# A first state in one transfer, low halves of w_out on GpSimd, and a new opening order in an attention-and-FFN kernel

## The chip, the cores and the metric

The kernel runs on one core of one Trainium2 chip. The metric is the device time of one execution in microseconds. A core has a tensor engine (TensorE, PE in the profile; PEld is its weight load), a vector engine (VectorE, DVE), a scalar engine (ScalarE, ACT), a Pool engine (GpSimd, POOL), and a queue that issues transfers (SyncE, SP). Each engine works off its own list in order and waits on semaphores for the others.

## What is computed

```python
def _attn_ref(x, state):  # (8, 8, 512, 64), (8, 8, 32, 64)
    scores = scale * np.matmul(x, state.transpose(0, 1, 3, 2))
    ...
    xread = np.matmul(a, state)
    scores2 = scale * np.matmul(state, x.transpose(0, 1, 3, 2))
    ...
    sread = np.matmul(a2, x)
    return np.concatenate([xread, sread], axis=2).astype(np.float32)

def _moe_ref(x, w_in, w_out):  # (4352, 512), (512, 2048), (2048, 512)
    h = x @ w_in
    relu6 = np.clip(h + 3.0, 0.0, 6.0)
    g = h * relu6 / 6.0
    return (g @ w_out).astype(np.float32)
```

Left out are the two softmaxes: that of `scores` over the 32 states of a head, that of `scores2` over its 512 tokens. The heads of the attention's result are laid side by side, so that 8 x 544 rows of 512 go through the feed-forward part. The two weights arrive as 64-bit floats, and the kernel turns their digits into 32-bit floats itself.

## The kernel before

**Stages.** For each of eight batches the kernel computes softmax weights of tokens over states, and a product w' of the state with `w_in` (function `wprime`, line 512 makes its matmuls), so that `a @ state @ w_in` becomes `a @ w'`. A step n of the main loop takes 128 of the 2048 hidden columns: `first(n)` multiplies w' with the weights into a PSUM bank `ps_h`, ScalarE (line 1027) and VectorE (line 1029) form g, and `second(n)`, two steps later, multiplies g with 128 rows of `w_out` into four accumulators `acc0` to `acc3`. Most products are made of three 32-bit products of high and low halves (line 967); `split` (lines 306 and 307) makes the halves: ScalarE rounds to the high half, VectorE subtracts. The very first step takes 32-bit operands as they are (`PLAIN = 1`): line 997 in `first`, line 1046 in `second`. A ninth pass over the state's own rows ends the kernel.

**Weights.** `weight()` loads a tile of 64-bit numbers (line 373) and decodes it: ScalarE casts the upper digits (`upper`, line 382), VectorE joins the lower ones (`join`, line 387). For `w_out`, ScalarE then rounds the high half (line 414) and VectorE subtracts for the low half (line 416). This happens once, mostly during the first batch.

**The opening, batch 0.** `load_x` issues x in four quarters of two heads (line 481), and behind the first `load_state` issues the state in two transfers of 32 KB, one for each of two groups of heads, in runs of 256 bytes (line 438). `take_in` turns the state on TensorE (line 593), copies it to `stT` on ScalarE (line 599), and spreads it over the zeroed `apart` in four VectorE copies (line 606); it turns each quarter of x (line 621, eight halves of 128 columns into one bank) and ScalarE copies it out (line 625). `tokens_by_rows` makes for each quarter q the scores (line 688), VectorE the maximum (699) and the difference (707), ScalarE the exponential (710), VectorE the sum (713). After each second quarter VectorE takes the reciprocal (718) and scales the pair (720). When all is scaled, TensorE turns the weights back in two groups of four (729), one copied out by ScalarE (731) and one by VectorE (732), and line 997 can begin.

**What sets the order.** Every piece of work is put into a `Plan` with its engine (T TensorE, V VectorE, S ScalarE, Q transfers), an assumed duration, a rank, what it reads and writes, and the buffers it holds. `order()` lays them out against assumed clocks; the first several hundred follow the list `OPENING`, by numbers in the order of `plan.add`. A transfer is assumed to land at `channel + 1.6`, where the channel starts 1.3 after the issue and moves 330 KB a microsecond. `issue()` emits the work in that order, and fills assumed gaps of TensorE before the first product with idle matmuls of a constant (line 1267), one for each 0.22 us until `WARM`, and one for each 0.13 after it; before `WARM` TensorE's work is assumed to take twice as long. In the list before, SP issues x quarter 0, the state, x quarter 1, a `w_out` tile, x quarters 3 and 2, then three transfers of `w_in` (two of one tile, one of two) and two of `w_out`.

Of the kernel before, what the change touches and what calls it, by code (L numbers as in the profile page):

```python
# [35 lines left out]
PLAIN = 1  # L36

# [31 lines left out]
class Plan:  # L69
# [5 lines left out]
    AFTER = {"T": 0.25, "V": 0.12, "S": 0.12, "Q": 0.0}  # L75
    WARM = 4.5
# [26 lines left out]
    def order(self):  # L103
# [13 lines left out]
        open_ops = {e: set() for e in "TVSQ"}  # L117
# [3 lines left out]
        clock = dict.fromkeys("TVSQ", 0.0)  # L121
# [4 lines left out]
        while len(row) < n_ops:  # L126
# [65 lines left out]
    def issue(self, tc, idle, until):  # L192

        with tc.manual_schedule(
            engines={ENGINE.PE, ENGINE.DVE, ENGINE.Activation, ENGINE.SP}
        ):
# [12 lines left out]
def tile_state_attention_then_hardswish_ffn(  # L209
# [8 lines left out]
    nc = tc.nc  # L218
# [35 lines left out]
    make_identity(nc, ident)  # L254
    three = cpool.tile([P, 1], F32, name="three")
# [32 lines left out]
    def S_(cost, rank, do, reads=(), writes=(), after=()):  # L288
        return plan.add("S", cost, rank, do, reads, writes, after)

# [48 lines left out]
    def weight(kind, k, n, place, rank, load_rank):  # L339
# [68 lines left out]
        def halves(rank):  # L408

            gone = [  # L410
                m for slot, users in plan.users.items() for m in users
                if slot[1] != "home" and slot[0] in (at_home["hi"][0][0], at_home["lo"][0][0])
            ]
            S_((0.6, 1.05)[n - 1], rank, lambda: nc.scalar.copy(w_out_of("hi", k, n), low()),
               lo_keys, at_home["hi"], gone)
            V(wide, rank, lambda: nc.vector.tensor_tensor(
                w_out_of("lo", k, n), low(),
                w_out_of("hi", k, n).bitcast(F32),
                op=ALU.subtract), [*lo_keys, *at_home["hi"]], at_home["lo"])
# [10 lines left out]
    first_exps = []  # L430

    def load_state(b, rank, after=()):
        key = ("st_raw", b)

        def load():
            raw = get(key, lambda: att.tile([P, NG, D], F32, name="st_raw", bufs=1))
            for u in range(NG):
                nc.sync.dma_start(raw[:, u, :], st_v[b, :, :, u, :])  # L438
# [149 lines left out]
    def take_in(b, rank, after=(), banks=None):  # L588
# [3 lines left out]
        if b < TURNED:  # L592
            T(0.12, rank[0], lambda: nc.tensor.transpose(
                bank(st)[:, :P], made["st_raw", b].rearrange("p u d -> p (u d)"), ident),
                [("st_raw", b)], [st], after)

        def put_state():
            stT = get(("stT", b), lambda: att.tile([P, P], F32, name="stT"))
            nc.scalar.copy(stT, bank(st)[:, :P])
        if b < TURNED:  # L600
            S_(0.22, RANKS["apart"] if b == 0 else URGENT, put_state, [st], [("stT", b)])
        for u in range(NG) if b < TURNED else ():
            for i in range(2):
                def put(u=u, i=i):
                    src = bank(st)[u * D : (u + 1) * D, :P].rearrange("p (q n) -> p q n", n=NS)
                    nc.vector.tensor_copy(apart[i * D : (i + 1) * D, :, u, i], src)
                V(0.22, RANKS["apart"] if b == 0 else URGENT, put, [st], [("apart", b, u, i)])
# [19 lines left out]
    def apart_parts(b):  # L627
        return [("apart", b, u, i) for u in range(NG) for i in range(2)]
# [39 lines left out]
    def tokens_by_rows(after, banks):  # L668
# [11 lines left out]
        for q in range(NQ):  # L680
# [20 lines left out]
            if q in ():  # L701
# [13 lines left out]
            if q % 2 == 0:  # L715
# [4 lines left out]
            V(0.62, r[4], lambda pair=pair, total=total: nc.vector.tensor_tensor(  # L720
                a_by_rows().rearrange("p (a q n) -> p a q n", q=NQ, n=NS)[:, :, pair], whole[:, :, pair, :NS],
                total(pair).unsqueeze(3).to_broadcast([P, A, NG, NS]), op=ALU.mult),
                [sum_key, (*bt_key, q - 1), part_key], [("w_in2", "a", "rows", q)])
        for g in range(NG):
            back = (banks[g], ("B", 0, g))

            def turn(back=back, g=g):
                for j in range(J):
                    nc.tensor.transpose(bank(back)[:, place(j)], a_by_rows()[:, place(j * NG + g)], ident)  # L729
            T(0.47, RANKS["turn0"][0], turn, [("w_in2", "a", "rows", q) for q in (1, 3)], [back], after)  # L730
            copy = (lambda g=g, back=back: nc.scalar.copy(a_first(g), bank(back)),
                    lambda g=g, back=back: nc.vector.tensor_copy(a_first(g), bank(back)))[g]
            (S_, V)[g](0.6, RANKS["turn0"][1 + g], copy, [back], [("w_in2", "a", g)])
# [7 lines left out]
    def halves_of_first(rank):  # L741
        for g in range(NG):
            split(rank, lambda g=g: made["aT", 0]["hi"]()[:, g], lambda g=g: made["aT", 0]["lo"]()[:, g],
                  lambda g=g: a_first(g), [("w_in2", "a", g)],
# [98 lines left out]
    def place(k):  # L843
        return slice(k * P, (k + 1) * P)
# [56 lines left out]
    def put(c, ps, cols):  # L901
# [3 lines left out]
            [n for k, n in scores_at.items() if k in (0, ("L", 0))])  # L905
# [66 lines left out]
    def first(n):  # L972
        b, i, _, _ = steps[n]
        ps = ("ps_h", n)
        if b < B:
# [8 lines left out]
            if plain(b, i):  # L984
                by_group = {g: [("w_in2", "a", g), (*PLAIN_WP, f0, g)] for g in wide}
# [312 lines left out]
```

## Time and profile before

| | |
|---|---|
| median of 3 runs | 647.14 us (646.94 to 649.2) |
| span of the profiled execution | 648.4 us |
| PE busy | 640.2 us, 99% |
| DVE busy | 393.1 us, 61% |
| ACT busy | 292.3 us, 45% |
| POOL busy | 1.3 us, 8 instructions |
| mean granted TensorE clock | 0.993 |

The profile is of one execution, whose span, 648.4 us, is its own time. Its times count from the start of the span. Busy times of TensorE are modelled ends of pipelined matmuls, so a busy TensorE may still be slow. The granted clock is a share of full speed. In a row of instructions, `xb<-in_x_dram` is written tile from read tile; a bracket or the last column tells how long the engine stood idle and what ended that. In a row of transfers the last number is the time from issue to landing.

### The profile page before, as it was taken

The numbers are of one execution on the slowest core, as the hardware profiler recorded it, in microseconds if no ns is written. First come the engines' busy times: TensorE is split into PE (matmuls) and PEld (weight loads), VectorE is DVE, ScalarE is ACT, GpSimd is POOL, SyncE is SP. The second block draws the span as 40 slices with busy tenths as digits, with TensorE's granted clock in tenths as the row PEclk, the third lists the DMA queues.
The fourth block names the chain that finished last, engine by engine and source line by source line (L and its number), as shares of the span: only waits on it lengthen the run. The fifth ranks groups of instructions, "written<-read, shape, count | busy, mean of one in ns | idle before, by whom it ended". The sixth has DMA issues, their size and how long they took to land.

```text
span 648.4 us, 9867 instructions
## 1 busy us (share of the span) xinstructions
PE 640.2 (99%) x3924; PEld 502.9 (78%) x3924; DVE 393.1 (61%) x678; ACT 292.3 (45%) x509; POOL 1.3 (0%) x8
## 2 busy tenths in 40 slices
PE   8999999999999999999999999999999999999997
PEld 7577778777878777787778787787778787888996
DVE  4989995387586356834595366834694444443552
ACT  3998664335344344534344344433353343433442
POOL 0000000000000000000000000000000000000000
PEclk7999999999999999999999999999999999999999
DMA  8789302644531405041231405050232001000101
GB/s 283 264 266 257 123 2 42 110 114 73 115 66 19 79 1 135 2 73 25 70 66 28 70 2 135 7 83 9 76 57 32 1 21 46 0 1 1 65 1 33
DMA packets 135270, 46.25 MB, mean 71 GB/s; under 512 B 123576, under 2 KB 129208, under 8 KB 135096
## 3 DMA queue, kind: packets, MB, share of 16 engines
q1 hardware_dynamic: 135224, 45.62, 29.1%
q8 instruction: 31, 0.51, 0.3%
q14 instruction: 15, 0.12, 0.1%
HBM read 33.02 MB, written 8.91 MB: 65 GB/s over the span
## 4 chain that ended last, share of the span: by engine, by line
PE 97%; DMA 1%; DVE 1%; SPq 0%; issue 0%; ACT 0%
PE acc L967 58%; PE ps_h L967 30%; PE ps_s L512 4%; PE ps_h L512 2%; PE ps_h L924 1%; DMA xb<-in_x_dram 1%; PE acc L1046 1%; PE ps_s L688 1%; PE acc L621 0%; PE ps_h L997 0%; SPq L438 0%; PE acc L688 0%; DVE w_in L720 0%; PE acc L729 0%; PE ps_s L924 0%; PE acc L512 0%
## 5 line engine op out<-in xcount | busy, mean ns | idle before, releaser
L967 PE MATMUL acc<-w_out_hi,g_hi 128*128 128x512 f32 x540 | 213.3, 395 | 0.0
L967 PE MATMUL acc<-w_out_lo,g_hi 128*128 128x512 f32 x540 | 210.5, 390 | 0.0
L967 PE MATMUL acc<-w_out_hi,g_lo 128*128 128x512 f32 x540 | 210.2, 389 | 0.0
L1027 ACT ACTIVATE g<-ps_h,three 128x512 f32<-128x512 f32 (+1 forms) x144 | 95.5, 665 | 225.7 <-PE ps_h L967 221.5
L1029 DVE SCALAR_TENSOR_TENSOR g<-g,ps_h 128x512 f32<-128x512 f32 (+1 forms) x144 | 94.5, 657 | 150.1 <-ACT g L1027 149.2
L967 PEld LDWEIGHTS acc<-w_out_hi,g_hi 128*128 128x128 f32 x540 | 101.4, 188 | 34.3 <-issue 13.0
L307 DVE TENSOR_TENSOR g_lo<-g,g_hi 128x512 fp32r<-128x512 f32 (+1 forms) x143 | 93.9, 658 | 52.2 <-ACT g_hi L306 51.0
L306 ACT CAST g_hi<-g 128x512 fp32r<-128x512 f32 (+1 forms) x143 | 85.2, 596 | 78.0 <-DVE g L1029 67.1
L967 PEld LDWEIGHTS acc<-w_out_hi,g_lo 128*128 128x128 f32 x540 | 101.4, 188 | 21.6
L967 PEld LDWEIGHTS acc<-w_out_lo,g_hi 128*128 128x128 f32 x540 | 101.5, 188 | 19.7
L967 PE MATMUL ps_h<-aT_hi,wp_hi 128*128 128x512 f32 (+1 forms) x246 | 89.8, 365 | 0.0
L967 PE MATMUL ps_h<-aT_lo,wp_hi 128*128 128x512 f32 (+1 forms) x246 | 89.0, 362 | 0.0
L967 PE MATMUL ps_h<-aT_hi,wp_lo 128*128 128x512 f32 (+1 forms) x246 | 89.0, 362 | 0.0
L967 PEld LDWEIGHTS ps_h<-aT_hi,wp_hi 128*128 128x128 f32 x246 | 46.4, 189 | 8.9 <-issue 0.8
L967 PEld LDWEIGHTS ps_h<-aT_lo,wp_hi 128*128 128x128 f32 x246 | 46.4, 189 | 7.8 <-issue 0.3
L967 PEld LDWEIGHTS ps_h<-aT_hi,wp_lo 128*128 128x128 f32 x246 | 46.4, 189 | 7.2
L967 PE MATMUL ps_h<-aT_hi,wp 128*128 128x512 f32 x144 | 50.2, 389 | 0.0
L967 PEld LDWEIGHTS ps_h<-aT_hi,wp 128*128 128x128 f32 x144 | 27.0, 188 | 5.6
L967 PE MATMUL ps_h<-aT_lo,wp 128*128 128x512 f32 x72 | 28.0, 389 | 0.0
L307 DVE TENSOR_TENSOR wp_lo<-ps_h,wp_hi 128x512 fp32r<-128x512 f32 x18 | 11.8, 686 | 12.3 <-ACT wp_hi L306 12.3
L512 PE MATMUL ps_s<-w_in,stT 64*32 64x512 f32 (+1 forms) x304 | 19.0, 556 | 0.0
L611 DVE STREAM_TRANSPOSE tmp<-raw 128x512 f32<-128x512 f32 x28 | 18.9, 694 | 0.0
(129 smaller groups left out, 438.3 us busy)
## 6 DMA issues: line engine op xcount, KB each, us to landing
xb<-in_x_dram SPq DMA_DIRECT2D x32, 256.0 KB, 4.0
out_dram<-ot SPq DMA_DIRECT2D x8, 1024.0 KB, 4.3
raw<-in_x_dram SPq DMA_DIRECT2D x112, 64.0 KB, 2.1
early<-in_moe_w_in_dram SPq DMA_DIRECT2D x5, 1023.0 KB, 6.7
raw<-raw SPq DMA_DIRECT2D x112, 32.0 KB, 2.0
raw<-in_moe_w_out_dram SPq DMA_DIRECT2D x7, 511.8 KB, 5.1
wide<-in_moe_w_out_dram SPq DMA_DIRECT2D x2, 1023.5 KB, 12.5
early<-in_moe_w_out_dram SPq DMA_DIRECT2D x2, 1023.5 KB, 8.4
```

The lines of the kernel that those rows point to most:

```text
L306: S_(cost, rank, lambda: nc.scalar.copy(hi(), src()), reads, [writes[0]])
L307: V(cost, rank, lambda: nc.vector.tensor_tensor(lo(), src(), hi().bitcast(F32), op=ALU.subtract), [*reads, writes[0]], [writes[1]])
L512: nc.tensor.matmul(out[u][cols, :], made["stT", b][rows, cols], moving(q)[rows], start=True, stop=True,)
L611: V(0.7, rank[0], lambda q=q, key=key: nc.vector.transpose(xT(b, q), made[key][:, q % 2]), [(*key, q % 2, u, k) for u in range(2) for k in ...
L688: nc.tensor.matmul(out[:, k, u], xT(0, q)[:, (u * 2 + k) * P : (u * 2 + k + 1) * P], apart[:, q, u], start=True, stop=True,)
L924: nc.tensor.matmul(bank(pr)[cols, u * D : (u + 1) * D], e2T(b, u)[:, j * P + q * NS : j * P + (q + 1) * NS], x_tile(b)[:, NG * q + u, j, : ...
L967: nc.tensor.matmul(ps, l, r, start=start and k == 0, stop=stop and k == n - 1)
L1027: S_(cost + 0.05, rank, lambda: nc.scalar.activation(g(), bank(ps)[:, :width], AF.Relu, bias=three), [ps], [g_key])
L1029: V(cost, rank, lambda: nc.vector.scalar_tensor_tensor(g(), g(), 6.0, bank(ps)[:, :width], op0=ALU.min, op1=ALU.mult), [ps], [g_key])
L1046: nc.tensor.matmul(bank(acc), made["g_hi", n][:, js], plain_out[i][1](), start=opens, stop=closes)
```

## The change

- The first state comes in one transfer of 512-byte runs: partition (h m) holds rows 2m and 2m+1 of head h, where before a partition held a row of each of two heads. The four copies into `apart` take their sources accordingly, and `stT` is then gathered from `apart` by two GpSimd copies (`together`) instead of one ScalarE copy.
- The low halves of `w_out` (line 416 before) are subtracted on GpSimd. The plan gets an engine P for it, with an assumed 1.35 us for 512 columns.
- At the end of the first softmax, the scaling of quarters 0 and 1 goes to GpSimd; that of 2 and 3 is made in two halves on VectorE. The weights are turned back in four groups of two, in four halves of two banks, and each half is copied out by an engine of its own: the first half of each group by ScalarE, the second by VectorE.
- The plan's assumptions: the channel starts 1.15 after the issue; the first five numbers land at `channel + 0.5` and the others at `+ 0.9`; `WARM` goes from 4.5 to 5.9; fewer idle matmuls are put into an early gap (`gap + 0.1` for `gap + 0.3`), more into a late one (`gap - 0.1` for `gap - 0.25`).
- A new list `OPENING`. Its transfers: x quarter 0, the state, x quarters 1 and 3, the first `w_in` tile, x quarter 2, the next `w_in` tile and the one of two, then two `w_out` tiles, of which the last is the one that stood behind x quarter 1. TensorE takes x quarter 3 before the first scores. A maximum of the scores of quarter 3 stands ahead of quarter 2's; the reciprocal of the first pair stands behind a join of `w_in`.
- `SUBTRACTED` is empty, so that `minus` gets no instruction.

```diff
-    WARM = 4.5
+    WARM = 5.9
...
+    first_loads = 5
...
-                channel = max(channel, t + 1.3) + size / self.transfer
-                done = channel + 1.6
+                channel = max(channel, t + 1.15) + size / self.transfer
+                done = channel + (0.5 if n < self.first_loads else 0.9)
...
-                        for _ in range(int((gap + 0.3) / 0.22) if last < self.WARM else int((gap - 0.25) / 0.13)):
+                        for _ in range(int((gap + 0.1) / 0.22) if last < self.WARM else int((gap - 0.1) / 0.13)):
...
-            V(wide, rank, lambda: nc.vector.tensor_tensor(
+            P_(1.35 * n, rank, lambda: nc.gpsimd.tensor_tensor(
                 w_out_of("lo", k, n), low(),
                 w_out_of("hi", k, n).bitcast(F32),
                 op=ALU.subtract), [*lo_keys, *at_home["hi"]], at_home["lo"])
...
-            raw = get(key, lambda: att.tile([P, NG, D], F32, name="st_raw", bufs=1))
-            for u in range(NG):
-                nc.sync.dma_start(raw[:, u, :], st_v[b, :, :, u, :])
+            raw = get(key, lambda: att.tile([P, NG * D], F32, name="st_raw", bufs=1))
+            nc.sync.dma_start(raw, state[b].rearrange("h (m r) d -> (h m) (r d)", r=2))
...
-            plan.add("Q", 1.39, rank, load, (), [key], after, 400.0)
+            plan.add("Q", 0.6, rank, load, (), [key], after, 80.0)
...
-        def put_state():
-            stT = get(("stT", b), lambda: att.tile([P, P], F32, name="stT"))
-            nc.scalar.copy(stT, bank(st)[:, :P])
...
+                    src = bank(st)[r * D : (r + 1) * D, :P].rearrange("p (q u m) -> p q u m", q=NQ, u=NG)
+                    dst = apart[i * D : (i + 1) * D, :, :, i].rearrange("p q u (m r) -> p q u m r", r=2)
+                    nc.vector.tensor_copy(dst[..., r], src)
...
+                nc.gpsimd.tensor_copy(
+                    stT[rows].rearrange("p (q n) -> p q n", n=NS), apart[rows, :, u, u])
...
+            early = q == 1
+            for h in range(1 if early else 2):
+                some = slice(0, A) if early else slice(h * A // 2, (h + 1) * A // 2)
...
+                (P_ if early else V)(
+                    1.3 if early else 0.35, r[4], scaled, [sum_key, (*bt_key, q - 1), part_key],
+                    [("w_in2", "a", "rows", q, h)])
...
+                T(0.24, RANKS["turn0"][0], turn, [("w_in2", "a", "rows", 1, 0), ("w_in2", "a", "rows", 3, h)], [back], after)
...
+                (S_, V)[h](0.36, RANKS["turn0"][1 + h], copy, [back], [("w_in2", "a", g, h)])
```

More of the change, by code (lines that the diff above doesn't have):

```diff
@@ L36 @@
 PLAIN = 1
+SUBTRACTED = ()
 OPENING = """
[25 rows of a table removed]
[24 rows of a table added]
 """
 class Plan:
-    AFTER = {"T": 0.25, "V": 0.12, "S": 0.12, "Q": 0.0}
-    WARM = 4.5
+    AFTER = {"T": 0.25, "V": 0.12, "S": 0.12, "P": 0.15, "Q": 0.0}
+    WARM = 5.9
+    first_loads = 5
     def __init__(self, slots, transfer):
@@ L116, in order @@
         ready = [0.0] * n_ops
-        open_ops = {e: set() for e in "TVSQ"}
+        open_ops = {e: set() for e in "TVSPQ"}
         for n in range(n_ops):
@@ L120, in order @@
                 open_ops[self.ops[n][0]].add(n)
-        clock = dict.fromkeys("TVSQ", 0.0)
+        clock = dict.fromkeys("TVSPQ", 0.0)
         clock["Q"] = clock["S"] = 0.7
@@ L194, in issue @@
         with tc.manual_schedule(
-            engines={ENGINE.PE, ENGINE.DVE, ENGINE.Activation, ENGINE.SP}
+            engines={ENGINE.PE, ENGINE.DVE, ENGINE.Activation, ENGINE.Pool, ENGINE.SP}
         ):
@@ L254, in tile_state_attention_then_hardswish_ffn @@
     make_identity(nc, ident)
+    minus = cpool.tile([P, P], F32, name="minus")
+    if SUBTRACTED:
+        nc.vector.tensor_scalar_mul(minus, ident, -1.0)
     three = cpool.tile([P, 1], F32, name="three")
@@ L289, in S_, with P_ @@
         return plan.add("S", cost, rank, do, reads, writes, after)
+    def P_(cost, rank, do, reads=(), writes=(), after=()):
+        return plan.add("P", cost, rank, do, reads, writes, after)
     def Q(rank, size, do, reads=(), writes=(), after=(), cost=0.53):
@@ L430, in tile_state_attention_then_hardswish_ffn @@
     first_exps = []
+    kept = []
     def load_state(b, rank, after=()):
@@ L593, in take_in, with put, together @@
             T(0.12, rank[0], lambda: nc.tensor.transpose(
-                bank(st)[:, :P], made["st_raw", b].rearrange("p u d -> p (u d)"), ident),
+                bank(st)[:, :P], made["st_raw", b], ident),
                 [("st_raw", b)], [st], after)
-        def put_state():
-            stT = get(("stT", b), lambda: att.tile([P, P], F32, name="stT"))
-            nc.scalar.copy(stT, bank(st)[:, :P])
-        if b < TURNED:
-            S_(0.22, RANKS["apart"] if b == 0 else URGENT, put_state, [st], [("stT", b)])
-        for u in range(NG) if b < TURNED else ():
[L603 to L607, printed above, removed]
+        for r in range(2) if b < TURNED else ():
+            for i in range(2):
+                def put(r=r, i=i):
+                    src = bank(st)[r * D : (r + 1) * D, :P].rearrange("p (q u m) -> p q u m", q=NQ, u=NG)
+                    dst = apart[i * D : (i + 1) * D, :, :, i].rearrange("p q u (m r) -> p q u m r", r=2)
+                    nc.vector.tensor_copy(dst[..., r], src)
+                V(0.22, RANKS["apart"] if b == 0 else URGENT, put, [st], [("apart", b, r, i)])
+        for u in range(NG) if b < TURNED else ():
+            def together(u=u):
+                rows = slice(u * D, (u + 1) * D)
+                stT = get(("stT", b), lambda: att.tile([P, P], F32, name="stT"))
+                nc.gpsimd.tensor_copy(
+                    stT[rows].rearrange("p (q n) -> p q n", n=NS), apart[rows, :, u, u])
+            kept.append(P_(0.3, RANKS["apart"], together, apart_parts(b), [("stT", b)]))
         for q in range(NQ):
@@ L627, in apart_parts @@
     def apart_parts(b):
-        return [("apart", b, u, i) for u in range(NG) for i in range(2)]
+        return [("apart", b, r, i) for r in range(2) for i in range(2)]
     def sums(b):
@@ L719, in tokens_by_rows @@
               [(*s1_key, q - 1)], [sum_key])
[L720 to L723, printed above, removed]
-        for g in range(NG):
[L725 to L733, printed above, removed]
+            early = q == 1
@@ new lines, in tokens_by_rows, with scaled @@
+            for h in range(1 if early else 2):
+                some = slice(0, A) if early else slice(h * A // 2, (h + 1) * A // 2)
+                def scaled(pair=pair, total=total, some=some, by=nc.gpsimd if early else nc.vector):
+                    by.tensor_tensor(
+                        a_by_rows().rearrange("p (a q n) -> p a q n", q=NQ, n=NS)[:, some, pair], whole[:, some, pair, :NS],
+                        total(pair).unsqueeze(3).to_broadcast([P, A, NG, NS])[:, some], op=ALU.mult)
+                (P_ if early else V)(
+                    1.3 if early else 0.35, r[4], scaled, [sum_key, (*bt_key, q - 1), part_key],
+                    [("w_in2", "a", "rows", q, h)])
@@ new lines, in tokens_by_rows, with turn @@
+        for g in range(NG):
+            for h in range(2):
+                back = (banks[h], ("B", 0, h), g)
+                js = range(h * J // 2, (h + 1) * J // 2)
+                cols = slice(g * S // 2, (g + 1) * S // 2)
+                def turn(back=back, g=g, js=js, cols=cols):
+                    for k, j in enumerate(js):
+                        nc.tensor.transpose(
+                            bank(back)[:, cols][:, place(k)], a_by_rows()[:, place(j * NG + g)], ident)
+                T(0.24, RANKS["turn0"][0], turn, [("w_in2", "a", "rows", 1, 0), ("w_in2", "a", "rows", 3, h)], [back], after)
+                there = lambda g=g, h=h: a_first(g)[:, h * S // 2 : (h + 1) * S // 2]
+                copy = (lambda there=there, back=back, cols=cols: nc.scalar.copy(there(), bank(back)[:, cols]),
+                        lambda there=there, back=back, cols=cols: nc.vector.tensor_copy(there(), bank(back)[:, cols]))[h]
+                (S_, V)[h](0.36, RANKS["turn0"][1 + h], copy, [back], [("w_in2", "a", g, h)])
@@ L743, in halves_of_first @@
             split(rank, lambda g=g: made["aT", 0]["hi"]()[:, g], lambda g=g: made["aT", 0]["lo"]()[:, g],
-                  lambda g=g: a_first(g), [("w_in2", "a", g)],
+                  lambda g=g: a_first(g), [("w_in2", "a", g, h) for h in range(2)],
                   [("aT", 0, g, "hi"), ("aT", 0, g, "lo")])
@@ L904, in put @@
             bank(ps)[:, cols].rearrange("p (q n) -> p q n", n=NS)), [ps], [("sread", c)],
-            [n for k, n in scores_at.items() if k in (0, ("L", 0))])
+            [n for k, n in scores_at.items() if k in (0, ("L", 0))] + kept)
     def tokens_read(b, tag="ps_s"):
@@ L984, in first @@
             if plain(b, i):
-                by_group = {g: [("w_in2", "a", g), (*PLAIN_WP, f0, g)] for g in wide}
+                by_group = {g: [*(("w_in2", "a", g, h) for h in range(2)), (*PLAIN_WP, f0, g)] for g in wide}
                 reads = [k for g in wide for k in by_group[g]]
```

2 lines of the change are left out of this document (1 added, 1 removed), and 49 rows, old and new, of the table OPENING.

## The prediction

> **What bounds the kernel now.** I read the page first, then the chain of waits in order of time, the stretches of the clock, the landings of the transfers, and the timeline of the first 25 us.
>
> ```profile
> span 648.4 us, 9867 instructions
> ...
> PE 97%; DMA 1%; DVE 1%; SPq 0%; issue 0%; ACT 0%
> ```
>
> The chain that ended last is TensorE for 97%. What is not TensorE lies at its beginning:
>
> ```profile
> 2.65 4.79 DMA xb<-in_x_dram
> ...
> 7.49 0.97 PE acc L621 x4
> 8.46 3.31 PE ps_s L688 x16
> 11.77 1.71 PE acc L621 x8
> ...
> 13.69 1.31 PE acc L688 x8
> ...
> 15.02 0.42 DVE m L699
> 15.44 0.60 DVE w_in L720
> ...
> 17.04 0.60 DVE w_in L387
> 17.64 0.69 DVE s L713 x2
> ...
> 18.34 0.27 DVE s L718
> ...
> 18.64 0.70 DVE w_in L720
> ...
> 19.47 1.06 PE acc L729 x8
> ...
> 20.92 1.91 PE ps_h L997 x4
> ```
>
> The columns are start, length, and what ran. The chain waits for the second quarter of x until 7.4, turns it (L621), computes the first scores (L688), ends the first softmax on VectorE (15.02 to 19.34), turns the weights back (L729), and at 20.9 begins the large products (L997). From there TensorE has no gap, as the row of 25 to 100 shows below with 75.00 us busy of 75.00. So the time is the moment at which L997 begins plus a fixed amount, and the change is worth what it moves that moment, unless a gap opens later.
>
> ```profile
> 3.00:4.00 1.00, 1.00 (x7) 0.69 (x6) 0.00 (x0) 0.00 (x0) 0.00 (x0) 1.00 0.38 81
> ...
> 4.28:7.70 3.42, 1.40 (x13) 1.06 (x12) 1.16 (x4) 0.78 (x2) 0.00 (x0) 1.00 0.97 301
> 7.70:14.52 6.82, 6.82 (x35) 6.73 (x33) 3.29 (x8) 3.54 (x7) 0.00 (x0) 0.50 1.04 367
> 14.52:20.85 6.33, 5.65 (x96) 3.88 (x95) 5.76 (x13) 4.00 (x10) 0.00 (x0) 1.00 0.35 137
> ...
> 25.00:100.00 75.00, 75.00 (x481) 55.22 (x480) 69.21 (x123) 57.64 (x103) 0.00 (x0) 1.00 0.60 178
> ```
>
> After the length stand the busy times of PE, PEld, DVE, ACT and POOL, then granted clock, DMA share, GB/s. Two things cost the opening. From 3 to 4 the DMA engines are at 0.38: only the state's small packets move. And from 7.70 to 14.52 TensorE has half its clock, right behind a stretch in which it worked 1.40 us of 3.42, because it waited for x.
>
> **The state in one transfer, x earlier.** One issue for two, and behind the state come the quarters of x in the order 0, 1, 3, then w_in's first tile, then quarter 2; a w_out tile of 512 KB that stood between quarters 1 and 3 goes to the end.
>
> ```profile
> xb<-in_x_dram SPq DMA_DIRECT2D x1, 256.0 KB, 2.7
> ...
> xb<-in_x_dram SPq DMA_DIRECT2D x1, 256.0 KB, 4.8
> ...
> xb<-in_x_dram SPq DMA_DIRECT2D x1, 256.0 KB, 5.7
> ```
>
> ```profile
> 0.74 0.45 SPq L481 DMA_DIRECT2D xb<-in_x_dram  x1
> 1.25 1.36 SPq L438 DMA_DIRECT2D st_raw<-in_state_dram  x2
> ...
> 19.95 3.12 SPq L373 DMA_DIRECT2D early<-in_moe_w_in_dram  x3
> ```
>
> The three landings are those of quarters 0, 1 and 3, counted from the start of the issue. One state issue costs between a half of 1.36 and the larger one in it, so about 0.65: quarter 1 is issued at 1.9, quarter 3 at 2.4, quarter 2 at 3.5 behind w_in's tile. Quarter 1 then lands between 1.9 + 2.7 = 4.6 (as quarter 0, with nothing ahead) and 1.9 + 4.8 = 6.7 (as now). I take 4.8, near the first, since what lay ahead of it was the state at 0.38 of the engines. Each 256 KB more takes 0.85 us at 301 GB/s: quarter 3 lands at 5.6 (at worst 2.4 + 5.7 = 8.1), w_in's tile at 7.3, quarter 2 at 8.2.
>
> The Trainium skill, "DMA: Bandwidth & Descriptors", section "Why a DMA increments its semaphore by 16 and not by 1", says that a transfer is spread over the largest number of engines up to 16 that divides the slowest dimension of both access patterns. The old source begins with q = 4 and the new one with 128 rows, so by it the state goes from four engines to 16 and the landing would be the early one; the 0.38 agrees as far as it goes.
>
> **TensorE up to the last scores.**
>
> ```profile
> 0.77 3.82 PE L1267 MATMUL ps_h<-const-bfloat16-1.0 128*128 128x256 bf16 x18 [0.77 <-PEq L1282]
> 4.43 0.60 PE L621 MATMUL acc<-ident,xb 128*128 128x128 f32 x4
> ...
> 7.49 0.97 PE L621 MATMUL acc<-ident,xb 128*128 128x128 f32 x4 [2.02 <-DMA xb<-in_x_dram]
> 8.25 3.52 PE L688 MATMUL ps_s<-sread_t,w_in 128*128 128x64 f32 x16
> ...
> 13.48 2.40 PE L688 MATMUL acc<-sread_t,w_in 128*128 128x64 f32 x16
> ```
>
> ```profile
> L606 DVE COPY sread_t<-ps_s 64x128 f32<-64x128 f32 x4 | 1.2, 289 | 3.7 <-PE ps_s L593 3.3 <-ACT stT L599 0.3
> L625 ACT COPY w_in<-acc 128x512 f32<-128x512 f32 x4 | 2.3, 586 | 6.7 <-PE acc L621 6.7
> ```
>
> The 18 idle matmuls delay the first turn: quarter 0 landed at 0.74 + 2.7 = 3.44, and TensorE, which works in order, came to it at 4.43. By the new formula the plan places the turn at 0.7 + 1.15 + 268/330 + 0.5 = 3.16, and int((3.16 - 0.6 + 0.1)/0.22) = 12 idle ones end at about 0.77 + 12 x 0.21 = 3.3. So quarter 0 is turned from 3.44, at the slow 0.97, to 4.4, the state to 4.65, quarter 1 from 4.8 to 5.8, quarter 3, between 0.60 and 0.97, to 6.6. The four copies that spread the state take 1.2 us of VectorE from 4.8 and end at 6.1, beside these turns. At 6.6 the scores begin, against 8.46.
>
> A set of eight score matmuls takes 3.52/2 = 1.76 at half clock. At full clock: of the 16 from 13.48 on, 14.52 - 13.48 = 1.04 us ran slow, that is 4.7 of them at 0.22, and 11.3 in the remaining 1.36 us, 0.12 each, so 0.96 a set. Two sets end at 8.5, the turn of quarter 2 (1.06/2 = 0.53, from L729) at 9.05, the third set at 10.0, the fourth at 11.0; its copy by ScalarE (0.59) lies beside the third. So the last scores are there at 11.0, where they now are at 15.0. Of these 4.0 us, 1.9 come from the earlier landing and 2.1 from the clock that is not lost.
>
> **The end of the first softmax.** From the last scores to the turn VectorE now works 15.02 to 19.34, 4.32 us. Out of that goes the scaling of the first pair (0.60, to GpSimd) and a maximum that the new order takes earlier (0.42); a reciprocal (0.27) comes in: 3.57. The first pair's scaling on GpSimd runs beside the sums, but is queued behind that late reciprocal, so a part of it may show. No row has such a GpSimd instruction:
>
> ```profile
> L264 POOL MEMSET sread_t<- 128x512 f32 x1 | 0.5, 531 | 0.0
> masks.py:199 POOL TENSOR_SCALAR_AFFINE_SELECT ident<-ident 128x128 f32<-128x128 f32 x1 | 0.3, 296 | 0.0
> ...
> L732 DVE COPY w_in<-acc 128x512 f32<-128x512 f32 x1 | 0.7, 692 | 0.0
> ...
> L382 ACT CAST tops<-early 128x512 f16<-128x512 bf16 x17 | 13.2, 787 | 1.3 <-DMA early<-in_moe_w_out_dram 1.3
> ```
>
> For 512 columns the bounds are 0.53 (a write alone) and 2.4 (four times 0.30 for one input, doubled for two); I take 1.3, nearer to the one-input row. Two sums, a reciprocal and the first half scaling (0.69 + 0.27 + 0.35) stand behind that reciprocal on VectorE, so 1.3 is just covered, and 2.4 would cost 1.1. I book 0.3. Behind the last half of the scaling the new order has a join of w_in (0.60) ahead of VectorE's half copy (half of L732's 0.69, 0.36 with its start); two of the eight transposes (1.06/4 = 0.27, after the 0.13 from 19.34 to 19.47) lie beside that join, and ScalarE's half copy too. So L997 begins at 11.0 + 0.02 + 3.57 + 0.3 + 0.60 + 0.36 + 0.13 = 16.0, where it began at 20.9: a gain of 4.9. The join needs its tile, the megabyte behind w_in's first two: 3.15 MB in all, of which 0.40 + 1.03 are moved by 7.70 (114 and 301 GB/s) and the rest at 367 GB/s by 12.4. With half a microsecond to land and two casts of 0.79 (L382) that is about 14.5, just before it is due at 14.9; a later tile moves L997 one for one. The w_out tile sent to the end is read no sooner than 1.91 us behind L997, at 17.9; 4.2 MB are moved by 15.2.
>
> **The low halves of w_out on GpSimd.**
>
> ```profile
> L416 DVE TENSOR_TENSOR w_out_lo<-raw,w_out_hi x7: 682/684/686, 29.6 to 97.1; 128x512 fp32r<-128x512 f32 x7
> L416 DVE TENSOR_TENSOR w_out_lo<-early,w_out_hi x3: 701/1215/1232, 37.6 to 70.3; 128x1024 fp32r<-128x1024 f32 x2, 128x512 fp32r<-128x512 f32 x1
> ...
> L416 DVE TENSOR_TENSOR w_out_lo<-wide,w_out_hi x2: 1216/1216/1216, 44.1 to 51.4; 128x1024 fp32r<-128x1024 f32 x2
> ```
>
> Twelve instructions, 16 tiles of 512 columns, 4.8 + 3.1 + 2.4 = 10.4 us, leave VectorE, and cost GpSimd 16 x 1.3 = 21 us (8 to 38 by the bounds) in the 75 us in which it does nothing now. I cost both at zero: TensorE is busy in all of that stretch, so VectorE's relief buys nothing, and a low half that is 0.6 to 1.4 us later is hidden by the steps between decoding and use. The tiny copies of the state by GpSimd instead of ScalarE are needed only after the last scores and are covered too.
>
> **Sum.** 648.4 - 4.9 = 643.5 for the profiled execution. That execution is 0.2% above the median of the runs, 647.14; taking the same 4.9 from that gives 642.2.
>
> **Rivals.** *The clock falls all the same (chance 0.14).* Between 4.28 and 7.70 TensorE was busy 1.40 us, and lost its clock. By my times it is busy about 3.2. If the clock is lost for the same 6.8 us nevertheless, three sets at 1.76 for 0.96 and a turn at 0.97 for 0.53 cost 2.8 and leave 2.1 of the gain. If quarter 1 also lands at its other bound, 6.7, the busy time is about 1.5 again, the scores begin at 8.7 and end near 15.2, and only the softmax's end is left, 0.7. So 645.0 to 646.4, and 645.7 in the middle; a landing near 5.7 decides. The second half of it is also the case in which the single transfer does not do what it says. Against it: 81 GB/s beside 301.
>
> *The start is given back (0.14).* Products that start 4.9 us sooner need their weights sooner, and the new plan allows less time for a landing. Half the gain lost is 644.6. Against it: the DMA engines stood at 0.35 from 14.52 to 20.85, 4.1 idle us, since the next w_in tiles were issued at 19.95, when slots came free; their slots' first tiles are decoded by about 12.5 now (the join stands a good microsecond behind the last scores), so the loads move forward as well.
>
> *GpSimd stops VectorE (0.10), the slower case.* VectorE has 75 - 69.2 = 5.8 us of idle time between 25 and 100. If it stands still during GpSimd's 16 tiles, at 1.6 us each (between my 1.3 and the bound of 2.4), that is 25.6 us for 10.4 freed and 5.8 spare: 9.4 late, and TensorE waits for the low halves of g (L307). Less the 4.9 gained it is 4.5 slower, 651.6. It decides at 21.1 us of standstill, 1.3 per tile with nothing running beside. The Trainium skill, "SBUF — State Buffer", section "Who interferes with whom", states such a lock: a VectorE instruction with two SBUF inputs and a GpSimd instruction that reads SBUF exclude each other for a whole instruction. That would hold for L387 and L307, but not for L1029, which reads PSUM, so it would be partial; no row here shows both at once.
>
> **How the numbers follow.** The forecast has 0.62. Its own range is 641.2 to 643.5: 1.0 better if quarters 1 and 3 land at the early bound, the turn of quarter 1 has the full clock (0.37) and GpSimd's scaling is hidden (0.3); 1.3 worse if that takes 2.4 (0.8 more) and the clock or a tile comes half a microsecond later. The range 641.1 to 646.2 takes in the first two rivals nearly whole and leaves out the third. Half a per cent, 3.2 us, is about what can be told from no change: faster is the forecast, 0.62; within it the first two rivals, 0.28; slower 0.10.
>
> **What would show it.** Right: one state issue, x quarter 1 landing before 5.3, clock 1.00 from about 5 on without a stretch of 0.50, L688 beginning before 7, L997's product before 17, the low halves on POOL with TensorE still busy 75 of 75 us. Wrong: a stretch at 0.50 after 7, or idle TensorE between 20 and 100 that ends with DVE L307 or a landing.

## The result and the profile after

The changed kernel takes 654.52 us (median of 4 runs: 651.68, 652.03, 657.02, 657.87); the kernel before took 647.04 in runs beside it (646.81 to 649.2). The ratio is 1.011, interval 1.008 to 1.015: slower by 7.5 us, where 4.9 us of gain were forecast. The profiled execution is the one of 651.68 us, with a span of 649.9; runs of this kernel last some 1.8 us longer than their span.

The page of after, its first line and the chain's shares:

```profile
span 649.9 us, 9876 instructions
...
PE 87%; DVE 6%; DMA 4%; issue 1%; ACT 1%; SPq 0%; DVEq 0%; ACTq 0%
```

The opening of after, from the timeline (start, length, engine, line, operation):

```profile
1.23 0.45 SPq L446 DMA_DIRECT2D st_raw<-in_state_dram  x1
...
3.69 1.09 PE L632 MATMUL acc<-ident,xb 128*128 128x128 f32 x4 [0.19 <-DMA xb<-in_x_dram]
...
5.57 0.66 PE L632 MATMUL acc<-ident,xb 128*128 128x128 f32 x4 [0.58 <-DMA xb<-in_x_dram]
...
7.09 1.90 PE L699 MATMUL ps_s<-sread_t,w_in 128*128 128x64 f32 x16
...
9.62 1.94 PE L699 MATMUL acc<-sread_t,w_in 128*128 128x64 f32 x16
...
13.62 1.05 POOL L736 TENSOR_TENSOR w_in<-ot,s 128x512 f32<-128x512 f32 x1 [6.54 <-DVE s L729]
...
16.69 1.02 PE L1020 MATMUL ps_h<-w_in,tmp 128*128 128x512 f32 x2
```

The opening came as forecast: one state issue, quarter 1 of x turned at 5.57, the scores from 7.09, and the first plain product (L997 before, L1020 now) at 16.69, which stood at 20.85. Nothing of the loss is here. It lies behind. Stretches of after, then the same of before (length, busy PE, PEld, DVE, ACT, POOL, clock, DMA share, GB/s):

```profile
5.06:16.69 11.63, 9.57 (x126) 7.64 (x127) 9.19 (x25) 7.20 (x17) 1.63 (x3) 1.00 0.99 347
25.00:100.00 75.00, 70.67 (x462) 51.62 (x461) 67.82 (x106) 54.09 (x97) 19.91 (x11) 1.00 0.53 156
...
33.00:41.00 8.00, 7.16 (x45) 5.36 (x44) 6.65 (x11) 7.26 (x12) 1.31 (x1) 1.00 0.40 108
49.00:57.00 8.00, 7.17 (x46) 5.33 (x45) 7.88 (x9) 5.83 (x11) 5.57 (x3) 1.00 0.87 270
73.00:81.00 8.00, 6.07 (x28) 4.71 (x26) 7.97 (x13) 3.50 (x6) 1.31 (x1) 1.00 0.00 0
```

```profile
33.00:41.00 8.00, 8.00 (x62) 5.84 (x47) 7.44 (x14) 6.85 (x14) 0.00 (x0) 1.00 0.69 229
49.00:57.00 8.00, 8.00 (x50) 6.00 (x49) 6.79 (x12) 6.93 (x13) 0.00 (x0) 1.00 1.02 204
73.00:81.00 8.00, 8.00 (x37) 6.63 (x36) 7.77 (x15) 5.17 (x10) 0.00 (x0) 1.00 0.34 98
```

TensorE, busy 75.00 of 75 us before, is now busy 70.67. The clock is full throughout, so it stands idle. From the first plain product to the end of the span it now takes 649.9 - 16.7 = 633.2 us, where before it took 648.4 - 20.85 = 627.6. Below I call this stretch the rest. Two places show what TensorE waits for. The chain of after, first around 36, with the issue ahead of it from the timeline:

```profile
18.81 11.57 DMA early<-in_moe_w_in_dram
...
30.46 0.78 ACT tops L390
...
31.84 0.69 DVE w_in L395
...
35.78 1.24 DVE w_in L395
...
37.16 0.67 PE ps_s L520 x16
```

```profile
18.27 0.51 SPq L381 DMA_DIRECT2D wide<-in_moe_w_out_dram  x1
```

A transfer of two `w_in` tiles, 8 and 9, issued at 18.81 behind a megabyte of `w_out`, lands at 30.4. The new list has tile 9 decoded first (cast at 30.46, which the plan placed at 27.4; join at 31.84), ahead of tiles 6 and 7, which TensorE needs next. Tile 7's join begins at 35.78, and L520 waits until 37.16. The other place is 73 to 81: VectorE is busy 7.97 of 8.00 us while the DMA engines move nothing, so there it is a pile on VectorE, not a transfer, that holds TensorE. A part of both waits is GpSimd. A join (L395) that takes 0.68 us alone takes longer beside a subtraction on GpSimd. Around 36 two joins take 1.84, of which the first ends at 37.02 by the chain above, 0.56 behind GpSimd; ahead of 73 one takes 2.30 and ends 0.55 behind it:

```profile
35.15 1.31 POOL L424 TENSOR_TENSOR w_out_lo<-early,w_out_hi 128x512 fp32r<-128x512 f32 x1 [8.48 <-ACT w_out_hi L422]
...
35.78 1.84 DVE L395 SCALAR_TENSOR_TENSOR w_in<-early,tops 128x512 uint32<-128x512 uint32 x2 [0.83 <-ACT tops L390]
```

```profile
70.08 2.45 POOL L424 TENSOR_TENSOR w_out_lo<-early,w_out_hi 128x1024 fp32r<-128x1024 f32 x1 [12.12 <-ACT w_out_hi L422]
...
70.78 2.30 DVE L395 SCALAR_TENSOR_TENSOR raw<-raw,tops 128x512 uint32<-128x512 uint32 x1
```

These rows show that VectorE is held, not what it costs in the end; that is what the first experiments ask.

### The profile page after: what moved, and what is told of

Same layout as the page of the kernel before. It is cut to its first block, busy times and chain, and to the rows that moved or that the text cites. A ratio compares the mean times of both kernels' runs of the same rounds, so it can differ in the third digit from the quotient of the medians.

```text
span 649.9 us, 9876 instructions
## 1 busy us (share of the span) xinstructions
PE 637.6 (98%) x3912; PEld 498.7 (77%) x3912; DVE 395.1 (61%) x667; ACT 292.8 (45%) x509; POOL 24.1 (4%) x23
## 4 chain that ended last, share of the span: by engine, by line
PE 87%; DVE 6%; DMA 4%; issue 1%; ACT 1%; SPq 0%; DVEq 0%; ACTq 0%
PE acc L990 52%; PE ps_h L990 27%; PE ps_s L520 3%; DMA early<-in_moe_w_in_dram 2%; PE ps_h L520 2%; PE ps_h L947 1%; DMA early<-in_moe_w_out_dram 1%; DMA xb<-in_x_dram 1%; DVE w_in L395 1%; DVE early L395 1%; DMA st_raw<-in_state_dram 0%; ACT tops L390 0%; DVE g_lo L315 0%; DVE wp_lo L315 0%; DVE g L1052 0%
## 5 line engine op out<-in xcount | busy, mean ns | idle before, releaser
L1052 DVE SCALAR_TENSOR_TENSOR g<-g,ps_h 128x512 f32<-128x512 f32 (+1 forms) x144 | 94.7, 658 | 152.9 <-ACT g L1050 152.0
L315 DVE TENSOR_TENSOR g_lo<-g,g_hi 128x512 fp32r<-128x512 f32 (+1 forms) x143 | 96.8, 677 | 50.8 <-ACT g_hi L314 49.3
L520 PE MATMUL ps_s<-w_in,stT 64*32 64x512 f32 (+1 forms) x304 | 19.5, 556 | 2.0 <-DVE w_in L395 1.7
L315 DVE TENSOR_TENSOR wp_lo<-ps_h,wp_hi 128x512 fp32r<-128x512 f32 x18 | 11.7, 685 | 11.1 <-ACT wp_hi L314 11.1
```

What stands on the lines that cost most here:

```text
L315: V(cost, rank, lambda: nc.vector.tensor_tensor(lo(), src(), hi().bitcast(F32), op=ALU.subtract), [*reads, writes[0]], [writes[1]])
L520: nc.tensor.matmul(out[u][cols, :], made["stT", b][rows, cols], moving(q)[rows], start=True, stop=True,)
L1052: V(cost, rank, lambda: nc.vector.scalar_tensor_tensor(g(), g(), 6.0, bank(ps)[:, :width], op0=ALU.min, op1=ALU.mult), [ps], [g_key])
```

## The experiments

First: is it GpSimd or the list? The low halves of `w_out` back on VectorE in the changed kernel, and alone on GpSimd in the old one, each with its own order written out to the last step, so that nothing else moves:

```diff
-            P_(1.35 * n, rank, lambda: nc.gpsimd.tensor_tensor(
+            V(wide, rank, lambda: nc.vector.tensor_tensor(
                 w_out_of("lo", k, n), low(),
```

> The changed kernel in its whole order, with only the twelve low halves of w_out back on VectorE. Theory G (GpSimd's instructions stop VectorE's two-input ones, 11.7 us of standstill counted in the trace, and free the load buffers late): the loss goes with them, 642 to 644. Theory L (the products start 4 us sooner than before, but the w_in and w_out tiles land no sooner, and the new order puts the megabyte that is needed last ahead of one needed first): VectorE's relief changes little, 649 to 652, with the landing of 11.6 us for w_in's fifth pair and TensorE idle before 40 as now.

> The kernel before in its whole order, with only the twelve low halves of w_out on GpSimd. Theory G: VectorE, with 5.8 us idle between 25 and 100, loses about 12 us of standstill for 10.4 us of work taken off, and buffers come free late: 650 to 654. Theory L: nothing else moves, so 646.5 to 648.

Measured: without GpSimd the changed kernel takes 656.11 us (651.0 to 657.01), ratio 1.012 (1.007 to 1.016), and a rest of 632.8 beside 633.2: as slow as with it. Its median lies above both expected ranges, because three of its four runs take 655.8 or more; the fourth, 651.0, is in the range of theory L. The old order with GpSimd takes 647.84, ratio 1.0005 (0.998 to 1.003), rest 628.6, as theory L had it. So GpSimd is not the main cause. The profile of the first held a surprise; its TensorE timeline and two stretches:

```profile
7.19 3.52 PE L766 MATMUL ps_s<-sread_t,w_in 128*128 128x64 f32 x16
...
11.35 3.51 PE L766 MATMUL acc<-sread_t,w_in 128*128 128x64 f32 x16
...
21.24 0.59 PE L1087 MATMUL ps_h<-w_in,tmp 128*128 128x512 f32 x1
```

```profile
2.89:6.30 3.41, 2.78 (x12) 1.82 (x11) 1.16 (x4) 0.59 (x1) 0.00 (x0) 1.00 0.87 252
6.30:19.95 13.65, 13.65 (x117) 11.34 (x116) 7.54 (x19) 6.13 (x14) 1.63 (x3) 1.00 0.79 274
```

Sixteen score matmuls take 3.52 us, as in the stretch of before whose clock was 0.50 (3.52 there), not 1.90 as in after: TensorE was cold until 19.95, where the record has its first change of clock. The clock column's 1.00 ahead of that is no measurement; the durations tell. The first product then begins at 21.24, 4.5 us late, with the very same opening. By this I explain the second pair of the changed kernel's runs, 657.0 and 657.9; of these two there is no trace.

Next, the parts that act on the opening: the new opening as far as the second plain product with the old order behind it (low halves on VectorE), and the old order with nothing but the state in one transfer (ScalarE spreads `stT` in four copies).

```diff
 OPENING: ... 95 107
-88 112 111 12 101 115 113 108
+14 12 13 227 96 88 112 111
```

> The changed kernel up to the first product, then the whole order of the kernel before, low halves on VectorE. If the early start can be kept at all (theory G, or theory L in its half that the new list is at fault), TensorE stays busy from 17 on and the time is 642.5 to 644.5. If the weights simply cannot be there sooner (the other half of theory L), TensorE idles between 25 and 60 and the time is 645.5 to 648.

```diff
-            for u in range(NG):
-                nc.sync.dma_start(raw[:, u, :], st_v[b, :, :, u, :])
+            nc.sync.dma_start(raw, state[b].rearrange("h (m r) d -> (h m) (r d)", r=2))
```

> The kernel before in its whole order, with only the first state in one transfer of 512-byte runs (its four spreads follow, and ScalarE copies it in four pieces). The second quarter of x should land near 5 instead of 7.45 and the granted clock should not fall to 0.50 after 7.7: the first large product begins 2 to 3.5 us sooner than at 20.9. Theory G says that this gain stays, 643.5 to 645. Theory L (weights cannot be there sooner): 645.5 to 647.

Measured: the first 648.5 (646.97 to 652.34), ratio 1.002 (0.9995 to 1.0045); its profile too was cold, first product 21.16, rest 628.9, so it missed both expected ranges. The second 646.89, ratio 1.000 (0.998 to 1.002), rest 627.6: the time of theory L, though not for its reason. Its timeline and stretches:

```profile
7.34 1.97 PE L758 MATMUL ps_s<-sread_t,w_in 128*128 128x64 f32 x16 [1.52 <-DVE sread_t L676]
...
17.47 0.70 PE L1067 MATMUL ps_h<-w_in,tmp 128*128 128x512 f32 x1
```

```profile
3.90:7.31 3.41, 1.93 (x17) 1.46 (x14) 1.16 (x4) 2.32 (x7) 0.00 (x0) 1.00 1.00 341
...
25.00:100.00 75.00, 75.00 (x488) 56.67 (x487) 67.91 (x118) 56.16 (x97) 0.00 (x0) 1.00 0.56 164
```

With the order of before and the clock kept, the first product begins at 17.47 and the span is 645.0, hence 646.8 us. The run with the old order and the low halves on GpSimd has the old opening unchanged, and kept its clock too:

```profile
6.34 0.66 PE L690 MATMUL acc<-ident,xb 128*128 128x128 f32 x4 [0.22 <-DMA xb<-in_x_dram]
7.25 1.97 PE L757 MATMUL ps_s<-sread_t,w_in 128*128 128x64 f32 x16 [0.26 <-DVE sread_t L675]
...
10.73 1.90 PE L757 MATMUL acc<-sread_t,w_in 128*128 128x64 f32 x16
...
17.78 1.98 PE L1066 MATMUL ps_h<-w_in,tmp 128*128 128x512 f32 x4
```

The kernel before has a median span of 645.0 to 645.7 in all later runs; its profiled 648.4 was an execution that had lost its clock. So the 20.85 from which my forecast counted was not the ordinary opening: 17.5 to 17.8 was. The single state transfer alone won nothing: quarter 1 is turned at 5.17 there, for 6.34, but the scores then wait 1.52 us for VectorE's spread of the state and begin at 7.34, for 7.25.

Then the clock by itself: five more idle matmuls in waits that the new opening has anyway, in the changed kernel, and in the mixture of new opening and old order.

```diff
+    MORE = {36: 3, 40: 2}
...
+                    for _ in range(self.MORE.get(n, 0)):
+                        idle()
```

> The changed kernel with nothing altered but five more idle matmuls on TensorE in waits that it has anyway: three ahead of the second turn of x, two ahead of the third. Theory (the twelve idle matmuls leave holes of 0.6 and 0.4 us, so that in some executions the granted clock does not rise until 20 us): the first plain product at 16.7 to 16.9 in every execution, the runs all at 651.5 to 652.5, none at 656 to 658, median 652. Rival (the runs at 657 have another cause, in the transfers): two groups as before, up to 658, median 652 to 657. Neither theory expects the stretch from the first plain product to the end to change: 633.

> The opening of the changed kernel up to its second plain product, then the order of the kernel before, low halves on VectorE, with the five more idle matmuls. Theory (clock kept up, old order behind): first product at 16.7 to 16.9, 628 to 629 from there, so a span of 645 to 646 and 646.5 to 647.5 in all runs, no different from the kernel before, which in executions that keep the clock begins at 17.5. Rival (the idle matmuls do not help): some runs at 651 to 652, median 648.5 as without them.

Measured: the changed kernel 651.27 us, all seven runs between 650.46 and 652.49, ratio 1.0056 (1.0036 to 1.0076), first product 16.72, rest 634.0. The mixture 647.76, twelve runs between 647.03 and 648.69, ratio 1.0005 (0.999 to 1.002), first product 16.77. In both, the runs some 5 us late are gone, and the changed kernel's median is 3.2 us lower of the 7.5. That twelve idle matmuls were too few is the likely reading, not a shown one: these runs were made on another chip than the two experiments with twelve, and the kernel before has late runs too, seven of 25 at 648.6 or more on the first chip and two of 18 on this one.

Is the rest lost by the order of the transfers? The first 40 transfers of the changed kernel behind its opening in the old order, and the mixture with the changed kernel's transfers (both with the five idle matmuls):

```diff
 OPENING: ... 95 107
-88 112 111 12 101
+14 96 162 88 112 111 12 101
```

> The changed kernel with the five idle matmuls, and the first 40 transfers after its opening in the order of the kernel before (state of the next batch with the first weights, out6 and out7 last); the order of all work on TensorE, VectorE, ScalarE and GpSimd is the changed kernel's. Theory (the new list loses its 5 us by the order of its transfers): from the first plain product to the end 628 to 629.5, time 647 to 648. Rival (it loses them by the order of its work on the engines, with the weights' decoding and the scores told too early or too late): 632 to 634, time 651 to 652. Shared: 630 to 631.

```diff
 OPENING (mixture): ... 95 107
-14 12 13 227 96 88 112 111
+12 13 227 88 112 111 101 108
```

> As the run with the changed kernel's opening, the old order behind it and five more idle matmuls, but with the first 40 transfers after the opening in the changed kernel's order (out6 ahead of in8, the state of the next batch among the last). Theory (the order of transfers costs the 5 us): 632 to 634 from the first plain product, 651 to 652 in all. Rival (the order of the work on the engines does): 628 to 629.5, 647 to 648.

Measured: 653.34 (ratio 1.008, 1.006 to 1.011), rest 634.7: no cure. And 656.74 (ratio 1.013, 1.011 to 1.016), rest 638.1: worse than either. Both sides missed. Two stretches of the first:

```profile
33.00:41.00 8.00, 7.98 (x54) 6.07 (x52) 6.03 (x11) 7.32 (x12) 2.19 (x2) 1.00 0.62 160
49.00:57.00 8.00, 5.86 (x39) 3.93 (x38) 4.67 (x8) 4.21 (x7) 3.45 (x3) 1.00 0.79 130
```

With tiles 8 and 9 issued ahead of that megabyte the wait at 36 is cured (7.98 for 7.16), but 2.1 us are lost at 49 to 57, where 0.8 were. In the second, a `w_in` tile came late altogether; its chain, and two stretches:

```profile
43.73 7.73 DMA early<-in_moe_w_in_dram
...
55.36 0.67 DVE w_in L465
...
56.17 1.11 PE ps_s L590 x16
```

```profile
51.00:56.00 5.00, 0.60 (x3) 0.17 (x1) 3.31 (x7) 4.46 (x8) 0.00 (x0) 0.90 0.69 92
55.01:61.84 6.83, 5.67 (x27) 3.93 (x28) 5.24 (x9) 5.57 (x10) 0.00 (x0) 0.50 0.92 283
```

TensorE worked 0.60 us of the 5 from 51 to 56 and then had half its clock for 6.83 us. Transfers and work are ordered for one another, and neither can be taken alone.

So I cut the new list: followed as far as a certain step, the old order behind it, low halves on VectorE, five idle matmuls. If one place lost the time, the rest would jump there.

```diff
 OPENING:
-the new list, all of its steps
+the new list to its step 129 (at 24.0 us), 196 (29.8), 244 (45.1), 342 (63.5); then the old order
```

> The changed kernel's list followed as far as the step that it places at 24.0 us, the order of the kernel before behind it; low halves on VectorE, five more idle matmuls. Cut at the second plain product, the same mixture had 628.9 from the first plain product to the end, with one hole of 1.59 us at 18.1. Theory (the loss of 5 us arises after 45 us, when VectorE has too much placed in 65 to 97): 627.6 to 629, time 646.0 to 647.5. Rival (it arises in the first 20 us behind the opening, where weights are placed too early or too late): 629.5 or more, time 648 or more.

> As the run cut at 24 us, but the changed kernel's list is followed to its step at 29.8 us. Theory (loss after 45 us): 627.6 to 629, time 646 to 647.5. Rival (loss in 20 to 45 us): 630 or more, time 648.5 or more.

> As the run cut at 24 us, but the changed kernel's list is followed to its step at 45.1 us, its transfers with it. Theory (loss after 45 us): 628 to 630, time 646.5 to 648.5, with TensorE's 0.8 us at 36 to 41 lost and no more. Rival (loss in 20 to 45 us, only showing later): 632 to 634, time 650.5 to 652.5.

> As the run cut at 24 us, but the changed kernel's list is followed to its step at 63.5 us. Theory (the order of VectorE's work from 65 to 97 us is what loses): 629 to 630.5, time 647.5 to 649. Rivals: the whole loss is laid by then, 632 to 634, time 650.5 to 652.5.

| new list as far as | first product | rest | median of the runs | ratio |
|---|---|---|---|---|
| 16 us (mixture above) | 16.77 | 628.9 | 647.76 | 1.0005 (0.999 to 1.002) |
| 24 us | 17.58 | 628.6 | 646.85 | 1.000 (0.999 to 1.001) |
| 30 us | 16.94 | 630.2 | 648.89 | 1.002 (1.001 to 1.0035) |
| 45 us | 16.72 | 631.1 | 649.89 | 1.004 (1.003 to 1.0055) |
| 63 us | 16.31 | 632.3 | 649.69 | 1.0036 (1.002 to 1.005) |

The stretch from 25 to 100 of the cuts at 24, 30, 45 and 63, one after the other:

```profile
25.00:100.00 75.00, 73.92 (x482) 55.40 (x481) 68.11 (x120) 56.51 (x102) 0.00 (x0) 1.00 0.57 164
```

```profile
25.00:100.00 75.00, 73.75 (x475) 53.93 (x474) 67.00 (x117) 55.56 (x100) 0.00 (x0) 1.00 0.56 158
```

```profile
25.00:100.00 75.00, 72.37 (x471) 53.27 (x470) 66.24 (x117) 54.80 (x99) 0.00 (x0) 1.00 0.53 155
```

```profile
25.00:100.00 75.00, 71.31 (x466) 52.09 (x465) 65.30 (x115) 54.56 (x97) 0.00 (x0) 1.00 0.53 153
```

My theory that the loss arises behind 45 us held for the cut at 24 and falls with the next: 2.5 of the rest are laid by 45 (628.6 to 631.1), another 1.2 by 63. No single place holds all of it. By the medians the largest step, 2.0, lies between the cuts at 24 and 30, and 1.0 more by 45; those at 45 and 63 are not told apart. The cut at 30 is the first that issues the megabyte of `w_out` ahead of tiles 8 and 9. TensorE's work in 25 to 100 falls too, but in other steps: 73.9, 73.8, 72.4, 71.3. The rests are of one execution each; that of the cut at 24 was 1.1 us above its median, and its 17.58 comes from a quarter of x that landed late.

Last, the two missing corners of list against engine, and a test of the clock in the kernel before, with nine idle matmuls in its wait from 5.5 to 7.5:

```diff
 (cut at 24 us)
-            V(wide, rank, lambda: nc.vector.tensor_tensor(
+            P_(1.35 * n, rank, lambda: nc.gpsimd.tensor_tensor(
```

> As the run that follows the new list to 24 us and the old order behind it, but with the low halves on GpSimd, as in the changed kernel: all edits of the change but its list behind 24 us. Theory (the list alone loses): 628.6 to 629.6 from the first plain product, 646.8 to 648.0. Rival (the low halves on GpSimd lose as soon as TensorE begins early): 631 to 633, 649.5 to 651.5.

The second is the whole new list with the edit of the first experiment and the five idle matmuls:

> The changed kernel's whole list with the low halves on VectorE and the five more idle matmuls: the fourth corner of the square of list and engine. Theory (the list loses whichever engine makes the low halves): 632 to 633.5 from the first plain product, 650.5 to 652, as with GpSimd (651.3). Rival (GpSimd is a part of the loss): 629.5 to 631, 648 to 649.5.

```diff
 (kernel before)
+    MORE = {35: 9}
```

> The kernel before, whole order, with nine more idle matmuls ahead of the second turn of x, in the wait of 2 us in which TensorE stood still from 5.5 to 7.5 when its clock fell. Theory (the runs of the kernel before at 649.7 to 651 are those in which the clock falls there, the profiled one among them, and the median has none of it): all runs at 646.4 to 647.6, median 646.8, unchanged. Rival (the clock's fall is in the median too): median 644 to 645.5.

| median us, ratio | low halves on VectorE | on GpSimd |
|---|---|---|
| old order behind 24 us | 646.85, 1.000 (0.999 to 1.001) | 648.03, 1.0016 (1.001 to 1.0025) |
| new list | 650.85, 1.006 (1.005 to 1.007) | 651.27, 1.0056 (1.004 to 1.008) |

The list costs 4.0 us with VectorE and 3.2 with GpSimd; GpSimd costs 1.2 in the old order behind 24 us, and the 0.4 in the new is within the intervals. The rows are from three chips, on which the kernel before had medians of 646.88 to 647.07. The kernel before with nine idle matmuls takes 647.47, ratio 1.0004 (0.999 to 1.002): its median holds no loss of the clock that could be won. One of its eleven runs was still at 650.17, as one or two in twenty of the kernel before are on these chips, so these few late runs are not settled by it.

## Why the prediction was wrong

**The sum's starting point.** I worked out 4.9 us from one execution and took them from the median: "taking the same 4.9 from that gives 642.2". That step failed. That execution had lost its clock in 7.70 to 14.52; executions that keep it begin their products at 17.5 to 17.8, not at 20.85. From there 16.7 is a gain of about 1. The two terms of the 4.0 us, 1.9 for the landing and 2.1 for the clock, were mostly not there to be won: with its clock kept the old opening begins the scores at 7.25 (7.09 after) and has the last ones done at 12.63 (11.56 after). The span of 648.4 beside a median of 647.14 was in view: with 1.8 us on top, the difference that later runs have, it was an execution of 650, well above the median.

**"The moment at which L997 begins plus a fixed amount."** That was the larger error. The amount went from 627.6 to 633.2. I had read the new list for the opening alone, and booked its remainder at nothing because TensorE was busy 75.00 of 75 us. But that was a property of the old order. The rival "the start is given back" had the mechanism, later weights, and half the price. My argument against it, loads that move forward, held for the issues, though the 19.95 in it is from the cold execution too: with the clock kept the old order issues its three `w_in` transfers at 16.89, 19.08 and 19.50, the changed kernel at 13.31, 17.84 and 18.81. It did not hold for the decoding: the list places its steps by landings that are assumed sooner (27.4 for 30.4), and an engine that works in order holds up what stands behind. That a late step in the list holds TensorE is shown at 36; that this is the whole of the loss is not.

**Twelve idle matmuls.** I took them as given by the formula, and used them for an earlier turn. The turn came early (3.69), but two of four runs are late, as the traced run of the same opening was whose clock did not rise. My rival on the clock asked whether it falls again after 7.70; that it might not rise at all I did not consider. Its price is larger, 4.5 us.

**The opening's end points were right** where the clock rose. Scores 7.09 for 6.6, last scores done at 11.56 for 11.0, product 16.69 for 16.0; most of the 0.7 is quarter 1, turned at 5.57 for 4.8. GpSimd's scaling took 1.05 for my 1.3.

**GpSimd at zero** was wrong by some 1 us behind the new opening with the old order (1.2 by the medians of two chips); in the kernel before (1.0005) and in the new list no cost is clear of the noise. The size of one subtraction was right, 1.30 for 1.3 (rows at the end). The lock of the third rival is there, in these rows of after:

```profile
41.29 2.45 POOL L424 TENSOR_TENSOR w_out_lo<-wide,w_out_hi 128x1024 fp32r<-128x1024 f32 x1 [4.83 <-ACT w_out_hi L422]
...
41.83 0.69 DVE L1052 SCALAR_TENSOR_TENSOR g<-g,ps_h 128x512 f32<-128x512 f32 x1 [1.15 <-ACT g L1050]
...
42.43 1.85 DVE L315 TENSOR_TENSOR g_lo<-g,g_hi 128x512 fp32r<-128x512 f32 x1
```

L315, 0.68 long when nothing runs beside it, lasts 1.85 and ends 0.54 behind GpSimd's end at 43.74; L1052, which reads PSUM, is not touched. This is what the Trainium skill, "SBUF — State Buffer", section "Who interferes with whom", says of two SBUF inputs; the trace agrees. The stretch of the corner of old order and GpSimd shows the sum:

```profile
25.00:100.00 75.00, 74.07 (x479) 54.75 (x478) 65.33 (x107) 56.60 (x101) 20.11 (x11) 1.00 0.56 158
```

VectorE's busy time is 65.33 beside 68.11 in the same order without GpSimd: 10.4 us were taken off it and 2.8 came free, so some 7.6 us of it is standing still. The rival's price was too high because it let all of GpSimd's time block and had VectorE wait for nothing else. That its 651.6 lies near the 651.27 of the changed kernel with the five idle matmuls is luck: with the low halves on VectorE the same list takes 650.85.

**The whole.** From 646.9: the opening with the clock kept and the old order, 646.85; GpSimd, 648.03 (+1.2); the new list, 651.27 (+3.2); executions that stay cold, 654.52 (+3.2). These are medians from different chips, on which the kernel before differs by up to 0.6 us, so only the sizes of the larger steps count, and the last rests on four runs. What stays open is which steps of the list cost most: most of the loss is laid by 45 us, and giving a single engine its old order was not tried, since the engines' orders depend on one another.

No version beat the kernel before: the best, the cut at 24 us and the state in one transfer, are equal to it.

## What to carry to other kernels

Before a gain is counted from a profiled execution, compare its own time with the median and look for a lost clock: what only that execution lost can't be won from the others. A list that orders all the work is one change from its first step to its last; an opening that starts earlier is worth nothing if the steps behind it are not ordered for it, and here a new order of the transfers alone cured nothing. Idle matmuls that raise the clock are to be counted in many runs, not in one: here two of the changed kernel's four runs were late with the same code.

## What the runs showed of the hardware

- A TensorE that the record calls busy need not by that raise its clock. In the changed kernel with the low halves on VectorE, from 6.30 to 19.95, busy 13.65 of 13.65 us with turns, scores, small products and, from 17.1 on, eight idle matmuls, it stayed at the cold durations. The Trainium skill, "TensorE: Matmul & The Clock Gate", section "What's actually happening", has the full clock after one busy window of some 3.4 us that runs by itself. The distance of the changes agrees (4.28, 7.70, 14.52 before: 3.4 and twice 3.4); "busy" in the sense of the record does not.
- The clock was kept through 3.41 us with 1.93 busy (3.90 to 7.31, state in one transfer), and lost after 3.42 with 1.40 busy (before, 4.28 to 7.70).
- A tiny VectorE instruction can be held by GpSimd as long as a large one, in after:

```profile
25.40 1.29 DVE L829 TENSOR_SCALAR nm<-nm 128x2 f32<-128x2 f32 x1
26.60 0.68 DVE L315 TENSOR_TENSOR g_lo<-g,g_hi 128x512 fp32r<-128x512 f32 x1
```

```profile
25.36 1.30 POOL L424 TENSOR_TENSOR w_out_lo<-raw,w_out_hi 128x512 fp32r<-128x512 f32 x1 [1.94 <-ACT w_out_hi L422]
```

Two elements in each partition took 1.29 us (0.17 in the kernel before), just as long as the subtraction that began 0.04 before it. In the corner of old order and GpSimd, another instruction of two elements (L909) took 2.33 us beside a subtraction of 2.45, and 0.15 in the same order without GpSimd.
